# Splitting the last products by token tile, and three smaller moves at the end of an attention and feed-forward kernel

## The chip, the cores and the metric

The kernel runs on one core of a Trainium2 chip. The metric is the time of one execution on the device, in microseconds. Before the change the median of three runs was 293.77 us (293.49 to 294.30). The profile is of one execution, whose span from first to last instruction was 291.8 us, at the full granted TensorE clock.

Engine names in the profile: PE is TensorE's matmul, PEld its weight load, DVE is VectorE, ACT is ScalarE, POOL is GpSimd, SP is SyncE, which issues most of the transfers. L530 is line 530 of the kernel as it was before.

## The reference

There are two stages. The first is attention over 4 batches and 8 heads, 768 tokens, head dimension 64, in which a query sees only the keys whose six projected sign bits are the same as its own:

```python
q_bits = (np.einsum('bhsd,dk->bhsk', q, proj) > 0)
k_bits = (np.einsum('bhsd,dk->bhsk', k, proj) > 0)
# bits -> bucket number
mask = q_bucket[:, :, :, None] == k_bucket[:, :, None, :]
scores = np.where(mask, scale * np.matmul(q, k.transpose(0, 1, 3, 2)), -1e9)
attn = softmax(scores)
attn_out = np.matmul(attn, v)
```

The second takes the result as 3072 tokens of 512 values through a feed-forward block with a hidden width of 2048:

```python
h = x @ w_in                         # 3072 x 2048
g = h * (1.0 / (1.0 + np.exp(-h)))
out = g @ w_out                      # 3072 x 512
```

## The kernel before

The main loop runs over 288 units of attention (nine for each head). A unit w issues the scores of unit w + 3, an exponential on ScalarE, and the products with v of unit w. Between them a queue of feed-forward units for the previous batch is worked off. The last batch's feed-forward block follows in `tail`, with what is left in the queue as its filler.

```python
def score(w):
    ...
    sp = ps.tile([P, 512], F32, tag="s", name="s_ps", bufs=LEAD)      # LEAD = 3
    ... matmuls, L381
    nc.scalar.activation(out=u, in_=sp, func=AF.Exp, scale=ESC)       # L384
```

PSUM tiles come from three groups: "s" (three banks, for the scores), "m" (three banks, for the first matmul's result h_ps and other things) and "o" (two banks). The feed-forward block of a batch is cut into a chunk of 512 tokens (ci = 0) and one of 256 (ci = 1). The second matmul uses seven products in place of eight (Strassen's scheme in Winograd's form), so operands are first combined by additions. A feed-forward unit of the first matmul:

```python
hp = ps.tile([P, 2, f, n // 2], F32, tag="m", name="h_ps", bufs=3)
... matmuls, L478
nc.scalar.activation(out=th, in_=hp, func=AF.Tanh, scale=0.5)         # L488
def g_op():
    nc.vector.scalar_tensor_tensor(out=g, in0=th, scalar=1.0, in1=hp, ...)   # L491
after.append(g_op)
```

The combinations, and the products with the chain tile that they open:

```python
def comb(ci, n, f):
    ...
    eng = nc.gpsimd if n > 2 and scoring else nc.vector
    eng.tensor_tensor(out=dst, in0=x, in1=y, op=op)                   # L513

def product(ci, n, t):
    ...
    first = t == 0 and n in (1, 6, 7)
    if first:
        banks[ci, bank] = ps.tile([P, nt, NC], F32, tag="m" if in_head else "s" if scoring else "o",
                                  name="o2_ps", bufs=3 if in_head or scoring else 2)
    ... eight matmuls, L530
    ... copied by ScalarE (L540), or added to an earlier part by VectorE (L542); store, L551
```

`scoring` is true in the loop and false in `tail`. `in_head` is true for the first eleven units of the later batches. Chain n=1 serves products 1 and 2, n=6 serves 6, 5 and 3, n=7 serves 7 and 4. In `tail` the first matmul of the last batch comes from L687 (products 1, 6, 2, 7, 5, 3, 4 for each block of the hidden width), with copies by ScalarE at L698, additions by VectorE at L701, silu by ScalarE at L704, and combinations at L713 to L723. Then come the last products, in `last`, for a larger chunk (ci = 0, two token tiles) and a smaller one (ci = 1, one token tile):

```python
def last(ci, n, t, c0=0, c1=NC):
    ...
    if c0:
        i = 4
    first = t == 0 and n in (1, 6, 7)
    if first:
        bank["o", ci, i] = ps.tile([P, nt, NC], F32, tag="o" if c0 else "ms"[ci], ...)
    op = bank["o", ci, i]
    for k in range(NK):
        nc.tensor.matmul(op[:, t, c0:c1], a[:, cs], y[:, k, c0:c1], ...)    # L793
    if t < nt - 1:
        return
    ...
        nc.scalar.copy(out=o, in_=op)                                       # L807
    ... or
        nc.vector.tensor_tensor(out=o[:, :, c0:c1], in0=op[:, :, c0:c1],
                                in1=kept[ci, with_part][:, :, c0:c1], op=ALU.add)   # L809
    ...
    nc.sync.dma_start(out=dst[:, 3 * r + t0 : 3 * r + t0 + nt, :], in_=o[:, :, c0:c1])  # L821

for n in (1, -1, 6, -2, 2, -6, 5, -5, 7, 3, -3, -7, 4, -4):
    for t in range(2 if n > 0 else 1):
        for cols in ((0, 192), (192, NC)) if n in (-7, -4) else ((0, NC),):
            last(int(n < 0), abs(n), t, *cols)
```

A negative n is the smaller chunk. The end of the kernel is therefore: product 4 of the larger chunk, both token tiles; then product 4 of the smaller chunk, first 192 columns and then 64.

Of the kernel before, what the change touches and what calls it, by code (L numbers as in the profile page):

```python
# [13 lines left out]
ALU = mybir.AluOpType  # L14
# [3 lines left out]
def kernel(  # L18
# [10 lines left out]
    nc = tc.nc  # L29
# [137 lines left out]
    NC = DMODEL // 2  # L167
# [286 lines left out]
    def flush():  # L454
        for fn in after:
            fn()
        after.clear()

    def moe_units(b):
# [4 lines left out]
        def mm1(ci, grp, dts=slice(0, NDT)):  # L464

            c0, n, f = ((0, 512, 1), (512, 256, 2))[ci]
            ft0 = grp * f
            half = ft0 // NK
            if (ci, half) not in blk:
                blk[ci, half] = gpl.tile([P, 2, NK, n // 2], F16, tag=f"g{ci}{half}", name="g",  # L470
                                         bufs=2 if (ci, half) == (0, 1) else 1)
            hp = opened.pop((ci, grp), None)
            if dts.start == 0:
                hp = ps.tile([P, 2, f, n // 2], F32, tag="m", name="h_ps", bufs=3)
            for j in range(f):
                ft = ft0 + j
                for dt in range(dts.start, dts.stop):
                    nc.tensor.matmul(hp[:, :, j, :], w_in16[:, dt, ft * P : (ft + 1) * P],  # L478
                                     xT[4 * b + dt][:, c0 : c0 + n]
                                     .rearrange("d (r c) -> d r c", r=2),  # L480
                                     start=(dt == 0), stop=(dt == NDT - 1))
            if dts.stop < NDT:
                opened[ci, grp] = hp
                return
            k0 = ft0 % NK
            g = blk[ci, half][:, :, k0 : k0 + f, :].rearrange("p r f c -> p r (f c)")
            th = thp.tile([P, 2, f, n // 2], F32, tag="th", name="th")
            nc.scalar.activation(out=th, in_=hp, func=AF.Tanh, scale=0.5)  # L488

            def g_op():  # L490
                nc.vector.scalar_tensor_tensor(  # L491
                    out=g,
                    in0=th.rearrange("p r f c -> p r (f c)"), scalar=1.0,
                    in1=hp.rearrange("p r f c -> p r (f c)"),
                    op0=ALU.add, op1=ALU.mult)

            after.append(g_op)

        def comb(ci, n, f):

            if n == 3 and (ci, 3) not in blk:
                w = blk[ci, 0].shape[-1]
                blk[ci, 3] = gpl.tile([P, NK, w], F16, tag=f"g{ci}d", name="gd", bufs=1)
            a11, a21 = blk[ci, 0][:, 0, f], blk[ci, 0][:, 1, f]
            a12, a22 = blk[ci, 1][:, 0, f], blk[ci, 1][:, 1, f]
            dst, x, y, op = {1: (a21, a21, a22, ALU.add),
                             2: (a11, a21, a11, ALU.subtract),
                             3: (blk.get((ci, 3)), a22, a11, ALU.subtract),
                             4: (a12, a12, a11, ALU.subtract)}[n]
            if n == 3:  # L510
                dst = dst[:, f]
            eng = nc.gpsimd if n > 2 and scoring else nc.vector
            eng.tensor_tensor(out=dst, in0=x, in1=y, op=op)  # L513

        banks, kept = {}, {}
# [53 lines left out]
        def then(fn, *combs):  # L569

            def unit():
                fn()
                for c in combs:
                    after.append(lambda c=c: comb(*c))
            return unit

        lo, hi, al = slice(0, NK // 2), slice(NK // 2, NK), slice(0, NK)
        first = [lambda grp=grp: mm1(0, grp) for grp in range(NFT)]
# [15 lines left out]
        if b == 0:  # L594
            one = [[lambda grp=grp, dt=dt: mm1(0, grp, slice(dt, dt + 1)) for grp in range(2)]
                   for dt in range(NDT)]
            first = one[0] + one[1] + one[2] + one[3] + first[2:]
# [10 lines left out]
    def moe_head():  # L608
        units, late[:6] = late[:6], []
        return units  # L610

    def moe_list(b):


        first, second, big, small = moe_units(b) if b else first_units
        if b == 0:
            units = first + spread(second, big[:8])
            late[:] = big[8:] + small
            return units
        units = spread(first[:-3], late) + [big[0]] + first[-3:] + [big[1]]  # L620
        for i, c in enumerate("ababaababababa"):
            units.append((second, big)["ab".index(c)][("ababaababababa"[:i].count(c)) + 2 * (c == "b")])
        late[:] = big[8:] + small
        return units
# [22 lines left out]
    def tail(fill):  # L647
# [16 lines left out]
        def gb(r, c, k, n=1):  # L664
            t = G[2 * (2 * r + c) + k // 4]
            return t[:, k % 4 * NR0 : (k % 4 + n) * NR0]
# [106 lines left out]
        kept = {}  # L773

        def last(ci, n, t, c0=0, c1=NC):

            nt, t0 = ((2, 0), (1, 2))[ci]
            i, x, y = {1: (1, (0, 0), B11), 2: (1, (0, 1), B21),
                       6: (2, 2, wt[2]), 5: (2, (1, 0), wt[1]), 3: (2, 4, B22),
                       7: (3, 3, B12), 4: (3, (1, 1), wt[4])}[n]  # L780
            if c0:
                i = 4
            first = t == 0 and n in (1, 6, 7)
            if first:
                bank["o", ci, i] = ps.tile([P, nt, NC], F32, tag="o" if c0 else "ms"[ci],
                                           name="o2_ps", bufs=2 if c0 else 3)
            op = bank["o", ci, i]
            cs = slice((t0 + t) * P, (t0 + t + 1) * P)
            for k in range(NK):
                a = {2: s2[:, k], 4: s4[:, k],  # L790
                     3: s3[k // 2][:, k % 2 * NR0 : (k % 2 + 1) * NR0]}[x] \
                    if isinstance(x, int) else gb(x[0], x[1], k)
                nc.tensor.matmul(op[:, t, c0:c1], a[:, cs], y[:, k, c0:c1],  # L793
                                 start=(first and k == 0), stop=True, skip_group_check=True)
            if t < nt - 1:
                return
            with_part = {1: None, 2: None, 6: 1, 5: 1, 3: 1, 7: 5, 4: 6}[n]
            keep = n in (1, 6, 5)
            pool = nrm if keep else ops
            if not keep and ci == 0:  # L800
                pool = thp
            if c0 == 0:
                bank["out"] = pool.tile([P, nt, NC], F32, tag=f"part{ci}{n}" if keep else ("th", "osb")[ci],
                                        name="osb", bufs=1 if keep else 3)
            o = bank["out"]
            if with_part is None:
                nc.scalar.copy(out=o, in_=op)  # L807
            else:
                nc.vector.tensor_tensor(out=o[:, :, c0:c1], in0=op[:, :, c0:c1],  # L809
                                        in1=kept[ci, with_part][:, :, c0:c1], op=ALU.add)  # L810
            if keep:
                kept[ci, n] = o
                return
            if ci and n == 7:
                if c1 < NC:
                    return
                c0 = 0
            r, c = {2: (0, 0), 3: (0, 1), 7: (1, 1), 4: (1, 0)}[n]
            dst = out[b * S : (b + 1) * S, c * NC + c0 : c * NC + c1].rearrange(
                "(p t) n -> p t n", p=P)  # L820
            nc.sync.dma_start(out=dst[:, 3 * r + t0 : 3 * r + t0 + nt, :], in_=o[:, :, c0:c1])  # L821

        for n in (1, -1, 6, -2, 2, -6, 5, -5, 7, 3, -3, -7, 4, -4):
            for t in range(2 if n > 0 else 1):
# [4 lines left out]
    NW = NH * NU  # L829
    BST = 8 * NU  # L830
# [106 lines left out]
    scoring = True  # L937
    in_head = False
    for w in range(LEAD):
        score(w)  # L940
    for w in range(NW):
        flush()
        for fn in at.pop(w, []):
            fn()
        if w % BST == 1:
            moeq.extend(moe_head())
        if w == BST + 5 or w % BST == 11 and w > 2 * BST:
            credit = 0.5
            moeq.extend(moe_list(w // BST - 1))
        keep = 3 if w >= NW - 12 else 0  # L950
        left = BST - w % BST
        n = -(-(len(moeq) - keep) // left) if len(moeq) > keep else 0
        in_head = w > 2 * BST and w % BST < 11
        credit += max(len(moeq) - keep, 0) / left
        skip = credit < 0.999 or w % QST in ((20, 21) if w > 2 * BST else (24, 25))
        if w > 2 * BST and w % BST < 11:
            skip = w % BST in (0, 2, 5, 7, 10)
        if n == 1 and len(moeq) - keep < left and skip:
            n = 0
        credit -= n  # L960
        for _ in range(n):
            moeq.popleft()()
        av(w)
        if w + LEAD < NW:
            score(w + LEAD)
# [3 lines left out]
    for w in sorted(at):  # L969
        for fn in at[w]:  # L970
            fn()
    scoring = False
    act = nrm.tile([P, 1], F32, tag="act", name="act", bufs=1)
    nc.scalar.activation(out=act, in_=sc[:, 0:1], func=AF.Silu)
    tail(late)
# [28 lines left out]
```

## Time and profile before

| what | us |
|---|---|
| median of three runs | 293.77 |
| span in the profile | 291.8 |
| TensorE busy | 285.8 |
| ScalarE busy | 224.7 |
| GpSimd busy | 204.3 |
| VectorE busy | 202.8 |

The busy time of an engine is its own; engines work side by side, and what sets the end is the chain of work in which each step waited for the one before. In order of time the end of the kernel reads so: the scores end about 236 us, the first matmul of the last batch (L687) runs from 243.9 to about 270 us with fillers between, the last products (L793) from 269.8 to 288.3 us, then the last additions and the last three stores. The stretches near the end, with the busy time of each engine:

```profile
core 0: us, PE busy (x) PEld busy (x) DVE busy (x) ACT busy (x) POOL busy (x), PEclk, DMA share, GB/s
248.00:270.00 22.00, 22.00 (x155) 14.93 (x153) 16.61 (x34) 18.80 (x39) 9.73 (x6) 1.00 0.09 28
270.00:288.00 18.00, 18.00 (x179) 16.30 (x177) 6.71 (x14) 3.31 (x6) 3.24 (x2) 1.00 0.23 75
288.00:292.00 4.00, 0.32 (x10) 0.20 (x7) 0.62 (x3) 0.00 (x0) 0.00 (x0) 1.00 0.32 98
```

Each line is a stretch, its length, then the busy time and number of instructions of TensorE's matmul, its weight load, VectorE, ScalarE and GpSimd, then the granted clock, and the share and rate of the transfers.

### The profile page before, as it was taken

Reading aid. Unit: us, or ns where it says so; the run is one execution under the profiler, and the core shown is the slowest. Engines: PE = TensorE matmul, PEld = TensorE weight load, DVE = VectorE, ACT = ScalarE, POOL = GpSimd, SP = SyncE. Lnnn points to the kernel's source line nnn. Section 1 sums busy time; section 2 is a strip of 40 time slices with the busy share of each in tenths; the row PEclk is TensorE's granted clock in tenths of the full one; section 3 lists DMA queues with packets and bytes.
Section 4 is the critical chain, followed back from the end, with each engine's and each line's share of the span. In section 5 each row is a group of like instructions: output and inputs, shape, how many; then the busy total and the mean of one; then the engine's idle time right before and its main releaser. Section 6 shows DMA issues by size and latency. Waiting matters only on the chain.

```text
span 291.8 us, 7761 instructions
## 1 busy us (share of the span) xinstructions
PE 285.8 (98%) x2934; PEld 196.7 (67%) x2934; DVE 202.8 (70%) x402; ACT 224.7 (77%) x428; POOL 204.3 (70%) x241
## 2 busy tenths in 40 slices
PE   8999999999999999999999999999999999999995
PEld 3666765555666665566666888656668887666884
DVE  6788869898887465854897446965657659777332
ACT  5999999998988687777887786878888855788400
POOL 8789999379997956999257991589999850254400
PEclk9999999999999999999999999999999999999999
DMA  6999997969979359872288226203020212101114
GB/s 197 244 238 210 235 151 117 235 86 150 197 120 213 85 88 226 155 136 55 72 178 122 50 66 167 80 21 48 26 47 0 65 29 82 46 3 36 38 67 133
DMA packets 105861, 32.91 MB, mean 113 GB/s; under 512 B 90912, under 2 KB 105312, under 8 KB 105824
## 3 DMA queue, kind: packets, MB, share of 16 engines
q1 hardware_dynamic: 101440, 28.23, 46.9%
q0 software_dynamic: 4224, 4.19, 9.7%
q8 instruction: 23, 0.38, 0.6%
q14 instruction: 14, 0.11, 0.1%
q10 hardware_dynamic: 160, 0.00, 0.0%
HBM read 27.27 MB, written 6.29 MB: 115 GB/s over the span
## 4 chain that ended last, share of the span: by engine, by line
PE 92%; DVE 3%; ACT 2%; issue 1%; POOL 0%; DVEq 0%; ACTq 0%; POOLq 0%
PE h_ps L478 21%; PE s_ps L381 20%; PE o_ps L530 13%; PE o_ps L413 12%; PE o_ps L793 6%; PE h_ps L687 5%; PE o_ps L560 5%; PE bp_ps L295 3%; ACT u L384 2%; PE tp_ps L199 2%; PE warm_ps L125 1%; PE bp_ps L315 1%; DVE tx L660 1%; DVE osb L542 1%; PE bp_ps L239 1%
## 5 line engine op out<-in xcount | busy, mean ns | idle before, releaser
L384 ACT ACTIVATE u<-s_ps 128x512 f16<-128x512 f32 x288 | 156.9, 608 | 27.7 <-PE s_ps L381 27.1
L413 PEld LDWEIGHTS <-u 128*128 128x128 f16 x1152 | 67.3, 98 | 38.1 <-ACT u L384 9.4
L413 PE MATMUL o_ps<-vv,u 128*128 128x65 f16 x1152 | 82.5, 194 | 0.6 <-ACT u L384 0.4
L478 PE MATMUL h_ps<-xT,win 128*128 128x512 f16 (+1 forms) x384 | 75.1, 326 | 0.0
L491 DVE SCALAR_TENSOR_TENSOR g<-th,h_ps 128x512 f16<-128x512 f32 x72 | 48.4, 680 | 36.9 <-ACT th L488 36.4
L381 PE MATMUL s_ps<-qkb 128*128 128x512 f16 x192 | 53.1, 326 | 0.2 <-ACT u L384 0.2
L381 PE MATMUL s_ps<-qka 128*128 128x512 f16 x192 | 52.5, 326 | 0.2 <-DVE qka L252 0.2
L488 ACT ACTIVATE th<-h_ps 128x512 f32<-128x512 f32 x72 | 43.8, 608 | 10.3 <-PE h_ps L478 7.1
L478 PEld LDWEIGHTS <-win 128*128 128x128 f16 x384 | 37.5, 98 | 17.5
L530 PEld LDWEIGHTS <-g 128*128 128x128 f16 x336 | 32.8, 98 | 7.0 <-issue 0.3
L433 POOL TENSOR_TENSOR x_pr<-osum,rec 128x384 f16<-128x384 f32 x23 | 19.7, 857 | 22.3 <-DVE rec L432 21.2
L265 POOL TENSOR_SCALAR qka<-qk 64x1536 f16<-64x1536 f32 x15 | 21.9, 1462 | 15.6 <-DVE qk L260 9.2
L265 POOL TENSOR_SCALAR qkb<-qk 64x1536 f16<-64x1536 f32 x15 | 22.0, 1469 | 1.2
L530 PE MATMUL o_ps<-wt,g 128*128 128x256 f16 x168 | 21.8, 272 | 0.1
L530 PE MATMUL o_ps<-wout,g 128*128 128x256 f16 x168 | 21.4, 273 | 0.0
L276 POOL TENSOR_TENSOR vsa<-v_sb 128x192 f32<-128x192 f32 x32 | 18.9, 591 | 0.0
L274 POOL CAST vv<-v_sb 128x384 f16<-128x384 f32 x32 | 16.7, 521 | 0.5
L560 PE MATMUL o_ps<-wout,g 128*128 128x512 f16 x64 | 16.4, 379 | 0.0
L717 POOL TENSOR_TENSOR gs<-qka,gs 128x768 f16<-128x768 f16 x2 | 3.3, 1644 | 18.5 <-ACT qka L704 15.7
L260 DVE STREAM_TRANSPOSE qk<-k_blk 128x768 f32<-128x768 f32 x10 | 16.0, 1598 | 0.0
L381 PEld LDWEIGHTS <-qka 128*128 128x128 f16 x192 | 15.4, 97 | 0.8 <-ACT qka L252 0.6
L260 DVE STREAM_TRANSPOSE qk<-q_blk 128x768 f32<-128x768 f32 x10 | 15.9, 1588 | 0.0
(123 smaller groups left out, 441.6 us busy)
## 6 DMA issues: line engine op xcount, KB each, us to landing
v_sb<-in_v_dram SPq DMA_DIRECT2D x15, 384.0 KB
out_dram<-osb SPq DMA_DIRECT2D x16, 256.0 KB
q_blk<-in_q_dram SPq DMA_DIRECT2D x40, 96.0 KB
k_blk<-in_k_dram SPq DMA_DIRECT2D x40, 96.0 KB
win<-in_moe_w_in_dram POOLq DMA_DIRECT2D x4, 512.0 KB, 7.7
wout<-in_moe_w_out_dram POOLq DMA_DIRECT2D x4, 512.0 KB, 6.7
q_sb<-in_q_dram SPq DMA_DIRECT2D x5, 384.0 KB
k_sb<-in_k_dram SPq DMA_DIRECT2D x5, 384.0 KB
```

The source lines that it names most:

```text
L260: nc.vector.transpose(out=dst, in_=qk_sb[p, "qk"[n]])
L265: nc.gpsimd.tensor_scalar(out=dst[rows, :], in0=qk32[p][rows, :], scalar1=CS, scalar2=1.0, op0=ALU.mult, op1=ALU.mult)
L276: nc.gpsimd.tensor_tensor(out=sa, in0=src[:, 0:3], in1=src[:, 3:6], op=ALU.add)
L381: nc.tensor.matmul(sp[:, o0 : o0 + n], t[:, S + jt * P : S + (jt + 1) * P], t[:, c0 : c0 + n], start=True, stop=True)
L384: nc.scalar.activation(out=u, in_=sp, func=AF.Exp, scale=ESC)
L413: nc.tensor.matmul(o_ps[h][:, c0 // P + i, :], u[:, o0 + i * P : o0 + (i + 1) * P], vv[:, jt, :], start=(not direct(h) and w % NU == 0 and ...
L433: (nc.vector if direct(h) else nc.gpsimd).tensor_tensor(out=x_pr[p][:, :, par * D : (par + 1) * D], in0=o[:, 0:NJ, 0:D], in1=rec[:, :, Non ...
L478: nc.tensor.matmul(hp[:, :, j, :], w_in16[:, dt, ft * P : (ft + 1) * P], xT[4 * b + dt][:, c0 : c0 + n] .rearrange("d (r c) -> d r c", r=2 ...
L488: nc.scalar.activation(out=th, in_=hp, func=AF.Tanh, scale=0.5)
L491: nc.vector.scalar_tensor_tensor(out=g, in0=th.rearrange("p r f c -> p r (f c)"), scalar=1.0, in1=hp.rearrange("p r f c -> p r (f c)"), op ...
L530: nc.tensor.matmul(op[:, t, :], x[:, k, t * P : (t + 1) * P], y[:, k], start=(first and k == 0), stop=True, skip_group_check=True)
L560: nc.tensor.matmul(op, x, w_out16[:, ft, :], start=(ft == 0), stop=(ft == NFT - 1))
```

## The change

It has four parts, all near the end of the kernel.

1. The last two groups of the larger chunk (products 7 and 4) get a bank for each token tile, so that VectorE can add token tile 0 while TensorE works on token tile 1. The store still takes both token tiles.
2. The store of the first 192 columns of the very last product is issued from ScalarE's queue; the last 64 columns stay on SyncE's.
3. Two combinations of the smaller chunk (n = 4 and n = 3) that fall into the tail are given to GpSimd, so that VectorE is free for the additions of the tail.
4. Product chains opened from unit 268 on take a bank of the first matmul's group and not of the scores' group.

```diff
-            eng = nc.gpsimd if n > 2 and scoring else nc.vector
+            eng = nc.gpsimd if n > 2 else nc.vector
 ... in last():
-            if c0:
+            split = ci == 0 and n in (7, 4)
+            if c0 or split and t:
                 i = 4
-            first = t == 0 and n in (1, 6, 7)
+            first = n in (1, 6, 7) and (t == 0 or split)
 ...
-            if t < nt - 1:
+            if t < nt - 1 and not split:
                 return
+            ts = slice(t, t + 1) if split else slice(0, nt)
 ...
-            if c0 == 0:
+            if c0 == 0 and ts.start == 0:
                 bank["out"] = pool.tile(...)
 ...
-                nc.vector.tensor_tensor(out=o[:, :, c0:c1], in0=op[:, :, c0:c1],
-                                        in1=kept[ci, with_part][:, :, c0:c1], op=ALU.add)
+                nc.vector.tensor_tensor(out=o[:, ts, c0:c1], in0=op[:, ts, c0:c1],
+                                        in1=kept[ci, with_part][:, ts, c0:c1], op=ALU.add)
 ...
-            if ci and n == 7:
-                if c1 < NC:
+            if n == 7 or split:
+                if ci and c1 < NC or split and t == 0:
                     return
-                c0 = 0
+                c0, ts = 0, slice(0, nt)
 ...
-            nc.sync.dma_start(out=dst[:, 3 * r + t0 : 3 * r + t0 + nt, :], in_=o[:, :, c0:c1])
+            (nc.scalar if (ci, n, c0) == (1, 4, 0) else nc.sync).dma_start(
+                out=dst[:, 3 * r + t0 + ts.start : 3 * r + t0 + ts.stop, :], in_=o[:, ts, c0:c1])
 ... in the main loop:
-        in_head = w > 2 * BST and w % BST < 11
+        in_head = w > 2 * BST and w % BST < 11 or w >= NW - 20        # NW - 20 = 268
 ... after it:
-    scoring = False
+    scoring = in_head = False
```

## The prediction

> **What bounds the kernel now.** I read the page's busy shares first: TensorE is busy for 285.8 us of a span of 291.8 us, so there is little idle time to win back, and the question is where exactly it lies. I then read the waits with TensorE as the waiter, then the chain of work that ended last from 222 us to the end, then the timeline around each place where that chain leaves TensorE, and last the stretches after the final product.
>
> ```profile
> PE 285.8 (98%) x2934; PEld 196.7 (67%) x2934; DVE 202.8 (70%) x402; ACT 224.7 (77%) x428; POOL 204.3 (70%) x241
> ...
> PE h_ps L687 <- DVE part L701: 0.4, 1, 0.4
> PE s_ps L381 <- ACT u L384: 0.2, 1, 0.2
> ```
>
> These two are the only waits of its matmuls after 222 us. The chain shows what led to each:
>
> ```profile
> 231.13 0.60 ACT th L488
> 231.73 0.50 ACT u L384
> 232.22 0.04 issue
> 232.27 0.38 PE s_ps L381 x2
> ...
> 246.12 0.46 DVE g L513
> 246.58 0.06 issue
> 246.63 0.27 DVE gd L513
> 246.90 0.34 issue
> 247.24 0.56 DVE part L701
> 247.80 0.04 issue
> 247.84 1.14 PE h_ps L687 x6
> ...
> 269.94 18.16 PE o_ps L793 x176
> 288.11 0.03 issue
> 288.13 0.35 DVE osb L809
> ```
>
> A score tile had to wait for an exponential, which stood behind a tanh in ScalarE's order. Later TensorE waited for VectorE's addition at L701, which stood behind the two combinations of L513. From 247.84 to 288.11 us the chain holds TensorE alone: what reaches TensorE earlier by 247.84 us reaches the end earlier. The last fence shows how much is lost at each place, and what follows the last product:
>
> ```profile
> 231.77 0.28 PE L413 MATMUL o_ps<-vv,u 128*128 128x65 f16 x4
> 232.27 0.38 PE L381 MATMUL s_ps<-qkb 128*128 128x256 f16 x2 [0.21 <-ACT u L384]
> ...
> 246.68 0.81 PE L687 MATMUL h_ps<-tx,sw 128*128 128x384 f16 x4
> 247.84 0.65 PE L687 MATMUL h_ps<-tx,sw 128*128 128x384 f16 x3 [0.35 <-DVE part L701]
> ...
> 288.24 0.38 SPq L821 DMA_DIRECT2D out_dram<-osb  x1
> ...
> 288.72 0.42 SPq L821 DMA_DIRECT2D out_dram<-osb  x1
> ```
>
> The reader should see that a bracket is less than the loss. Matmuls overlap, so the cadence counts. Four of the 65-column products take 0.12 us in the chain: the score could have begun at 231.77 + 0.12 = 231.89 and began at 232.27, a loss of 0.38 us. Four 384-column products follow one another by 0.65 us (246.03 to 246.68 in the timeline): the next could have begun at 246.68 + 0.65 = 247.33 and began at 247.84, a loss of 0.51 us.
>
> [...] from 289.1 to 290.4 us the DMA share is 0.87 to 1.08 in each tenth (but the first, 0.40) at up to 369 GB/s, so the three last stores already fill the engines. [...] the combination that begins at 223.38 us, while GpSimd runs L645, takes 2.61 us, where those after 246 us with GpSimd idle take 0.68; the additions of L701, one input from PSUM, take 0.51 us each from 253.56 us beside GpSimd's L717. [...]
>
> **The change part by part.**
>
> Chains from unit 268. Working through the queue of the loop, I find three product chains of the last sequence: chain n=1 opens at unit 259, before the new limit; n=6 opens at unit 276; n=7 opens only in the tail. So one tile alone changes its bank. It opens at 228.51 us and is freed by the addition of n=3, at 242.44 + 0.68 = 243.12 us. Before, it takes one of three score banks, so only two scores can be in flight, and the score at 232.27 must wait for the exponential two before it (231.62 to about 232.2). With three, it needs the one before that, done at 230.99. Gain: 0.38 us. The cost would be in the first matmul: it keeps two banks instead of three until 243 us. Its tiles begin at 230.06, 234.03, 236.87 and 238.61 us; each needs the tile two before it to have been read by L491. Those reads end at about 229.04, 229.69, 232.94 and 236.42 us, each earlier than needed, by 1.0 us at the least. The opening itself needs a bank whose L491 ends at 227.58, 0.9 us early. So no new wait: 0.
>
> Two combinations on GpSimd. The only ones with n over 2 outside the scoring are those of the smaller chunk, n=4 and n=3, each 128x1024. They cost VectorE 0.68 us each, begun at 246.04 and 246.63. L701 then begins when product 2 of the first block ends, near 246.5, and ends near 247.1, before 247.33. That frees all 0.51 us. But the next bound is near: two products later TensorE needs bank 1 after ScalarE's copy (247.53 to 248.01), and would be there at 247.33 + 0.65 = 247.98. With the 0.04 us of a hand-over (the step at 247.80 in the chain), it starts at 248.05, so 0.07 us goes back. Gain: 0.51 - 0.07 = 0.44 us. GpSimd takes 2.12 us for each (the median of its L513 row), together 4.24, from about 245.2 to 249.5 us in the new order. Its next work is at 253.17, and the products that read the results come at 261.56 and 264.06. Both have room.
>
> Last products by token tile. TensorE does the same matmuls. VectorE does two additions of 128x256 (0.425 us each) instead of one of 128x512 (0.691), twice: 0.16 us more each, in a stretch in which it is busy 6.7 of 18 us. For n=7 nothing waits. For n=4 the last addition now takes 0.425 instead of 0.691, so the 256 KB store can be issued 0.27 us sooner: at about 287.97 instead of 288.24. Its own fourth bank of the matmul group was freed by the copy ending at 277.56, and is wanted at 281.13: no wait.
>
> Two queues. Before, issues begin at 288.24, 288.72 and 289.23 us. With the 96 KB store on ScalarE's queue, I expect 287.97, about 288.5 and about 288.65. The data flow from 289.15 to 290.42 us without a break. They move 384 KB in 1.27 us, so an earlier last issue doesn't shorten them; the flow's start is what counts, and that is the 0.27 us of the split. For the second queue I take 0.
>
> Sum: 0.38 + 0.44 + 0.27 = 1.09 us. The time is 293.77 - 1.09 = 292.68, which I state as 292.7 us.
>
> **The rivals.**
>
> First, the banks: with n=6 in a matmul bank, the first matmul of the smaller chunk could be what waits. For it: VectorE's reads of h_ps at L491 wait for the tanh by up to 2.4 us over the whole span, and a combination beside GpSimd took 2.61 us; one such delay in 229 to 236 us would use up the 1.0 us of room. Against it: the four dates above. It would give back up to 0.4 us: 293.1.
>
> Second, GpSimd stands in VectorE's way: a combination running into one of VectorE's with two SBUF inputs would lengthen that to as much as 2.6 us, and L713 to L715 feed silu's blocks and the last products. For it: the 2.61 us above. Against it: the tx combinations end by 245.52 (about 245.1 in the new order), where GpSimd begins, and L713 comes at 251.47 (about 250.7), over 1 us after GpSimd ends. If it happened: 0.5 to 1.5 us lost, 293.2 to 294.2.
>
> Third, the end is set elsewhere: the span ends 1.4 us after the last data, in completion that none of this touches, and the second queue may begin its flow later than expected, or have a longer completion. Then the end's 0.27 us is lost: 292.95. Or the issue does count, because the last 32 KB flow alone and slowly (41 to 244 GB/s in the last three tenths); then up to 0.3 us more is gained: 292.4.
>
> Fourth, a freed wait comes back: TensorE gets ahead and meets the next late producer. In the blocks after 250 us it meets the copy of ScalarE once in each, with about 0.08 us (253.48 + 8 x 0.1625 = 254.78, begun at 254.86); that is in the trace already and moves along. I see no other within 0.1 us.
>
> **Range and chances.** All three gains together are 0.4% of the time; no part can bring or cost 2% (5.9 us) by anything in the trace. The spread of the three times is 0.8 us, so the median may be off by 0.3 either way. Half of the gains lost gives 293.2; the end gaining 0.3 more gives 292.4. I take 292.1 to 293.4. Chances: 0.01 faster by over 2%, 0.98 within, 0.01 slower.
>
> **What would show each step.** Right: no wait of TensorE for u on the score line near 232 us, and none for part at L701 near 247; L513 in that place on GpSimd with about 2.1 us each; L701 beginning directly after product 2; the products of L793 beginning about 0.8 us earlier than 269.78; the last data flow beginning about 0.27 us nearer to the last product, still without a break, and about as long. Wrong: a TensorE wait on h_ps for L491, VectorE operations of 1 us or more between 245 and 252 us, a gap in the last flow, or a span that shrinks while TensorE's idle time does not.

## The result and the profile after

The changed kernel takes 292.58 us (median of six runs, 292.28 to 292.96), against 293.65 us before (six runs): 1.07 us less, a ratio of 0.9958 with a 95% interval of 0.9943 to 0.9973. In the table of busy times only GpSimd's has moved by more than 1 us, by the two combinations that it took over (204.3 to 208.5 us):

```profile
PE 285.7 (98%) x2934; PEld 196.7 (68%) x2934; DVE 202.3 (70%) x402; ACT 224.7 (77%) x428; POOL 208.5 (72%) x243
```

The chain of work that ended last, of the changed kernel (start, length, engine, tile, line):

```profile
232.00 0.21 PE s_ps L381
232.21 0.12 PE o_ps L413 x4
232.34 0.22 PE s_ps L381 x2
...
245.45 3.00 PE h_ps L687 x18
...
269.42 18.16 PE o_ps L794 x176
287.58 0.02 issue
287.60 0.36 DVE osb L811
```

Before, this chain left TensorE twice after 222 us, near 232 and between 239.7 and 247.8 us. Now it doesn't leave it at all before the last addition: the 18 products of L687 from 245.45 us on follow one another through the place where TensorE had stood still, and no matmul after 222 us has a wait in the list of waits. L794, L811 and L823 are the earlier L793, L809 and L821. The timeline of the changed kernel shows how:

```profile
245.53 2.13 POOL L513 TENSOR_TENSOR g<-g 128x1024 f16<-128x1024 f16 x1 [7.80 <-PE o_ps L530]
...
246.53 1.02 DVE L701 TENSOR_TENSOR part<-h_ps,part 128x384 f32<-128x384 f32 x2 [0.50 <-PE h_ps L687]
246.58 1.46 PE L687 MATMUL h_ps<-tx,sw 128*128 128x384 f16 x8
...
247.96 0.48 PE L687 MATMUL h_ps<-xT,sw 128*128 128x384 f16 x2
...
286.94 0.42 DVE L811 TENSOR_TENSOR osb<-o_ps,osb 128x256 f32<-128x256 f32 x1 [0.39 <-PE o_ps L794]
```

L701 now waits for TensorE, and not TensorE for L701. The eight products of 0.1625 us each would end their turn at 246.58 + 1.30 = 247.88, and the next begins at 247.96: the 0.08 us that ScalarE's copy costs in each block. The last line is the addition of token tile 1 alone, 0.42 us long.

One caution in comparing the two profiles by the clock: TensorE reaches the product with v ahead of the first of these places at 232.05 us here and at 231.77 before, so 0.28 us were lost earlier in this execution, where the program hasn't changed. I therefore compare distances between instructions, not dates. From this product with v to the first of the last products (L793, now L794) it is 269.78 - 231.77 = 38.01 us before and 269.25 - 232.05 = 37.20 us now, 0.81 us less, where the prediction's first two terms are 0.82; in a second profile of the changed kernel it is 37.20 us again. The spans (291.8 and 291.0 us) differ by only 0.8 because of the 0.28 us; that of the second profile was 290.6 us.

### The profile page after: what moved, and what is told of

Read it like the earlier page. It is cut to its first block, busy times and chain, and to the rows that moved or that the text cites. A ratio compares the mean times of both kernels' runs of the same rounds, so it can differ in the third digit from the quotient of the medians.

```text
span 291.0 us, 7769 instructions
## 1 busy us (share of the span) xinstructions
PE 285.7 (98%) x2934; PEld 196.7 (68%) x2934; DVE 202.3 (70%) x402; ACT 224.7 (77%) x428; POOL 208.5 (72%) x243
## 4 chain that ended last, share of the span: by engine, by line
PE 95%; ACT 2%; issue 1%; DVE 1%; POOL 0%; DVEq 0%; ACTq 0%; POOLq 0%
PE h_ps L478 21%; PE s_ps L381 20%; PE o_ps L530 15%; PE o_ps L413 13%; PE h_ps L687 6%; PE o_ps L794 6%; PE o_ps L560 5%; PE bp_ps L295 3%; ACT u L384 2%; PE tp_ps L199 2%; PE warm_ps L125 1%; PE bp_ps L315 1%; PE bp_ps L239 1%; PE tp_ps L212 1%; PE o_ps L404 0%
## 5 line engine op out<-in xcount | busy, mean ns | idle before, releaser
L513 POOL TENSOR_TENSOR g<-g 128x1024 f16<-128x1024 f16 x7 | 15.2, 2188 | 7.8 <-PE o_ps L530 7.8
L701 DVE TENSOR_TENSOR part<-h_ps,part 128x384 f32<-128x384 f32 x24 | 12.6, 555 | 5.1 <-PE h_ps L687 3.0
```

## The experiments

### Each part alone

Four kernels took one part of the change each.

Banks alone:

```diff
-        in_head = w > 2 * BST and w % BST < 11
+        in_head = w > 2 * BST and w % BST < 11 or w >= NW - 20
-    scoring = False
+    scoring = in_head = False
```

> Only the fourth part: chains from unit 268 take a matmul bank. My theory (three separate waits, each worth its own term): TensorE's wait for u near 232 us is gone, the wait for part at L701 near 247 us stays with its loss of 0.51 us, the last flow of stores starts as long after the last product as before; 0.38 us less than before, about 293.3 against 293.65. Rival (the freed wait comes back in another place, since h_ps has one bank less): a TensorE wait for L491 between 230 and 239 us, and 0 to 0.1 us less than before.

Measured: 293.17 us (21 runs), ratio 0.9987 (0.9979 to 0.9996). The list of TensorE's waits after 200 us has one line left, the one near 247 us:

```profile
PE h_ps L687 <- DVE part L701: 0.3, 1, 0.3
```

In the timeline the product with v is followed by the score after 0.12 us, where it took 0.50 before (231.77 to 232.27): 0.38 us gained, as expected, and no wait in another place.

```profile
231.65 0.29 PE L413 MATMUL o_ps<-vv,u 128*128 128x65 f16 x4
231.77 0.38 PE L381 MATMUL s_ps<-qkb 128*128 128x256 f16 x2
```

The rival of the lost matmul bank falls.

Combinations alone:

```diff
-            eng = nc.gpsimd if n > 2 and scoring else nc.vector
+            eng = nc.gpsimd if n > 2 else nc.vector
```

> Only the third part: two tail combinations on GpSimd. My theory: the wait near 247 us is gone, and the block that follows starts 0.44 us sooner with 0.07 us of the 0.51 going to ScalarE's copy; the wait near 232 us stays; 0.44 us less than before, about 293.2. Rival (GpSimd hinders VectorE): operations of VectorE of 1 us or more between 245 and 250 us and 0.2 us gained at most.

Measured: 293.33 us (13 runs), ratio 0.9987 (0.9978 to 0.9996). Here the other line is left:

```profile
PE s_ps L381 <- ACT u L384: 0.2, 1, 0.2
```

The same stretch of TensorE, from the first products of L687 with tx to the first with xT after them, takes 247.52 to 248.90 = 1.38 us; before it took 246.68 to 248.49 = 1.81. That is 0.43 us gained. In this kernel, and then the end of the stretch before:

```profile
247.52 1.46 PE L687 MATMUL h_ps<-tx,sw 128*128 128x384 f16 x8
248.90 0.48 PE L687 MATMUL h_ps<-xT,sw 128*128 128x384 f16 x2
...
248.49 0.49 PE L687 MATMUL h_ps<-xT,sw 128*128 128x384 f16 x2
```

VectorE's additions beside the two GpSimd operations (246.46 to 250.68 us) take 1.02 us for two, as without them.

Split alone, with all stores on one queue:

```diff
+            split = ci == 0 and n in (7, 4)
 ... (the other lines of the change in last(), but not the ScalarE queue)
```

> Only the first part: products 7 and 4 of the larger chunk by token tile, all stores on one queue. My theory: the flow of the last stores is bound by its start, so it starts 0.27 to 0.32 us nearer to the last product and takes about as long as before (1.27 us); both waits of TensorE stay; 0.3 us less than before, about 293.35. Rival (the last issue counts): without the second queue the last issue still comes about 1.1 us after the last product's end, the flow gets a gap or a thin end, and nothing or 0.1 us is gained.

Measured: 293.30 us (13 runs), ratio 0.9994 (0.9985 to 1.0002). By the times alone this isn't clear of nothing; by the profile the end has moved, see the table below.

Two queues alone:

```diff
-            nc.sync.dma_start(out=dst[:, 3 * r + t0 : 3 * r + t0 + nt, :], in_=o[:, :, c0:c1])
+            (nc.scalar if (ci, n, c0) == (1, 4, 0) else nc.sync).dma_start(
+                out=dst[:, 3 * r + t0 : 3 * r + t0 + nt, :], in_=o[:, :, c0:c1])
```

> Only the second part: the 96 KB store on ScalarE's queue. My theory: the last issue moves from 289.23 to about 288.72 us, but the flow starts at the same distance from the last product and moves the same 384 KB, so nothing is gained: 0 to 0.06 us. Rival (the last issue sets the end): up to 0.3 us less than before.

Measured: 293.58 us (13 runs), ratio 1.0001 (0.9993 to 1.0009). Nothing gained, as expected.

For the end of the kernel I take as zero the begin of VectorE's addition of the last 192 columns (the last VectorE step of the chain: 288.13 us before, 287.60 us in the changed kernel). The trace says when the last data packet ends, which stretches of 0.01 us show too, and when the last instruction of the core ends:

| kernel | data stop, us after zero | core ends, us after zero |
|---|---|---|
| before | 2.36 | 3.67 |
| changed | 2.04 | 3.37 |
| split alone, one queue | 2.05 | 3.36 |
| two queues alone | 2.37 | 3.67 |

The split moves the end of the data by 0.32 us and the end of the core by 0.31; the second queue moves neither by more than 0.01, with the split or without it. In all four the data flow without a gap for about 1.36 us. The first of the last three stores is issued at 288.24 us before, 0.11 us after zero, and in the changed kernel 0.21 us before zero:

```profile
287.39 1.06 SPq L823 DMA_DIRECT2D out_dram<-osb  x2
```

The kernels of this set shared 49 runs of before. Medians are 0.46, 0.30, 0.33 and 0.05 us below theirs (293.63), together 1.14. The runs of one kernel spread over 0.6 to 1.1 us (all but one of those of before), so the median depends a little on where they happen to fall; the lowest runs (before 293.39; 293.03, 292.95, 293.09, 293.40) give 0.36, 0.44, 0.30 and -0.01, together 1.09. Either sum is close to the change's 1.07. The times alone don't resolve more than that: the ratios above multiply to 0.9969, about 0.9 us, and 0.9958 of the whole change is within their joint uncertainty. That the parts add rests on the distances in the profiles: 0.38, 0.43 and 0.31 us one by one, and 0.81 (the first two) and 0.31 us together.

### Does it matter where the GpSimd operations lie?

The changed kernel with one more tail combination on GpSimd:

```diff
-            eng = nc.gpsimd if n > 2 else nc.vector
+            eng = nc.gpsimd if n > 2 or n == 2 and not scoring else nc.vector
```

> The changed kernel with a third tail combination (n = 2 of the smaller chunk) on GpSimd too. It begins about 241.7 us, just before VectorE's eight combinations tx (L660), which have two inputs in SBUF; the two that the change moved begin after tx is done. If where they lie decides (my theory): tx is held up until GpSimd is done, about 243.9 us, the blocks of L687 that read tx wait, and 0.4 to 1.0 us of the gain is lost: 293.0 to 293.6. Rival (a GpSimd operation does not hinder VectorE, or VectorE has room here): tx ends as before or sooner, and the time is that of the changed kernel, 292.6, within 0.1.

Measured: 298.64 us (4 runs), ratio 1.0164 (1.0151 to 1.0177). The direction is the expected one, the size is not: about 6 us above the changed kernel, not 0.4 to 1.0. The timeline of this kernel, first GpSimd, then VectorE, then TensorE:

```profile
241.37 2.13 POOL L513 TENSOR_TENSOR g<-g 128x1024 f16<-128x1024 f16 x1 [4.04 <-DVE g L513]
245.18 2.12 POOL L513 TENSOR_TENSOR g<-g 128x1024 f16<-128x1024 f16 x1 [1.69 <-PE o_ps L530]
247.26 2.23 POOL L513 TENSOR_TENSOR gd<-g 128x1024 f16<-128x1024 f16 x1
...
242.41 1.30 DVE L660 TENSOR_TENSOR tx<-xT 128x384 f16<-128x384 f16 x1
...
245.21 2.30 DVE L660 TENSOR_TENSOR tx<-xT 128x384 f16<-128x384 f16 x1
247.44 2.27 DVE L660 TENSOR_TENSOR tx<-xT,tx 128x384 f16<-128x384 f16 x1
...
250.82 1.40 PE L687 MATMUL h_ps<-tx,sw 128*128 128x384 f16 x4 [2.61 <-DVE part L701]
```

A tx combination takes 0.35 us elsewhere in this trace. The first is held until 243.71, just after the added GpSimd operation ends at 243.50. That pushes the last two back into the two operations that the change had moved, which begin 0.03 and 0.18 us ahead of them. All three end 0.21 or 0.22 us after the GpSimd operation beside them, and take 1.30, 2.30 and 2.27 us. Both inputs of a tx combination are in SBUF. The additions of L701, with one input from PSUM, weren't lengthened by GpSimd: two take 1.02 us beside it in the changed kernel, and 1.02 us with GpSimd idle here (255.19 us). What holds the one kind and not the other, no trace shows. L701 comes after the tx combinations in VectorE's order, and TensorE waits for it.

The second half of the loss is in the windows of the same kernel (length, then busy time of TensorE's matmul, weight load, VectorE, ScalarE and GpSimd, then the granted clock):

```profile
247.50:250.90 3.40, 0.72 (x4) 0.36 (x4) 3.40 (x5) 0.48 (x1) 1.99 (x1) 1.00 0.00 0
250.90:254.30 3.40, 3.40 (x14) 1.99 (x14) 1.36 (x3) 1.70 (x3) 0.00 (x0) 0.50 0.35 116
254.30:256.00 1.70, 1.70 (x13) 1.01 (x12) 0.81 (x2) 1.13 (x3) 0.00 (x0) 1.00 0.00 0
```

After the stall TensorE's granted clock is 0.50 for 3.4 us: 14 matmuls fill 3.40 us there, and 13 the 1.70 us that follow at 1.00. By the distance from the first product of L687 with tx to the one that waited for L701, it lost 4.0 us to waiting (5.95 us, 244.87 to 250.82, against 1.95 in the changed kernel: 245.28 to 246.58 + 0.65). Half the clock for 3.4 us is 1.7 us more, an estimate from the granted clock. Together 5.7 us. In the profiles the way from that first product to the first of L794 is 5.78 us longer than in the changed kernel (244.87 to 274.62 against 245.28 to 269.25); the medians differ by 6.06.

### Is one matmul bank less ever felt?

The changed kernel with the limit brought down by 41 units, so that every chain of the last sequence that opens in the loop takes a matmul bank:

```diff
-        ... or w >= NW - 20
+        ... or w >= NW - 61
```

> The changed kernel with the limit of unit 268 brought down to unit 227, so that all chains of the last sequence take a bank of the first matmul's group. It asks whether one bank less for h_ps costs anything. My theory: chains at unit 229 to 259 hold a bank while VectorE is behind (a combination of 1.4 to 2.6 us beside GpSimd near 222 to 226 us), so a wait of TensorE for L491 shows up there, 0.2 to 0.8 us in all: 292.8 to 293.4. Rival (two banks are enough everywhere): no wait, and as fast as the changed kernel, 292.6 within 0.1.

Measured: 292.67 us (5 runs), ratio 0.9964 (0.9952 to 0.9976). My expectation was wrong and its rival right: TensorE has no wait after 200 us in this kernel either, and the time is the changed kernel's. In this run two banks were enough for h_ps in all of the last sequence.

### A shorter end?

If the last flow is bound by its 384 KB, it should help to store token tile 0 of product 4 as soon as it is added. In both kernels below the larger chunk's product 4 is stored in two pieces of 128 KB; the first is called e7 in the expectations, and the second also keeps all stores on SyncE's queue.

```diff
-            if n == 7 or split:
+            if n == 7:
                 if ci and c1 < NC or split and t == 0:
                     return
```

> The changed kernel with product 4 of the larger chunk stored by token tile too, 128 KB each, the last stores on two queues. My theory: the last flow was bound by its 384 KB; with 128 KB of them gone before the last product it is bound by the last issue: it ends about 0.9 us after the issue at 0.5 us behind the last product, some 0.3 to 0.4 us sooner than in the changed kernel: 292.2 to 292.3. Rival (the end is set by the completion after the last issue, whatever it moves): less than 0.15 us gained.

> As e7, but with all stores on one queue. If the amount of data no longer binds (my theory), the last issue now counts: it comes about 0.4 to 0.5 us later than with two queues, so 0.3 to 0.5 us of time more than e7, about 292.6. Rival (the second queue never counts): as e7 within 0.1 us.

Measured: 292.86 us (22 runs, ratio 0.9976, 0.9966 to 0.9986) and 292.90 us (22 runs, 0.9974, 0.9962 to 0.9985). Neither is faster than the changed kernel, and the queue again makes no difference in the time, as the rival of the second expectation had it. I ran the changed kernel, the first of these again and two more on one chip. The two more join the last 96 KB and 32 KB into one store of 128 KB, with product 4 of the larger chunk stored whole, and by token tile:

```diff
 ... one store at the end:
-            if n == 7 or split:
+            if n == 7 or split or ci and n == 4:
 ... one store at the end, and product 4 by token tile:
-            if n == 7 or split:
+            if n == 7 or ci and n == 4:
```

> The changed kernel again, on the same chip as the three that follow: about 1.1 us less than before, 0.9962; the last data end about 1.97 us after VectorE's addition of the last 192 columns begins, and the core's end follows about 1.4 us later.

> e7 again (product 4 of the larger chunk stored by token tile), beside the changed kernel on one chip. In e7 the data ended sooner (1.82 us after that addition begins) but the end of the core followed 1.77 us after them, not 1.4. If that belongs to the kernel (stores whose data do not queue behind others take as long from issue to completion anyway), it is seen again, and the time is 0.1 to 0.3 us above the changed kernel's. If it was chance, the end follows after 1.4 us and the time is 0.15 us below.

> The changed kernel with the two last stores (96 KB and 32 KB) made one of 128 KB, issued by ScalarE after the addition of the last 64 columns. Two issues are left at the end. If the amount of data and the last issue set the end: data end about 1.8 us after the addition of 192 columns begins, 0.15 us less time than the changed kernel. If the completion of small stores costs (the 32 KB in rows of 256 bytes): up to 0.4 us less. If the earlier start of the 96 KB counts: as the changed kernel or up to 0.2 us more.

> Both: product 4 of the larger chunk stored by token tile, and one 128 KB store at the end. If the completion after a gap in the flow is what made e7 slow, it is as slow here as e7 or more, 0.1 to 0.3 us above the changed kernel; if the thin last store did it, it is 0.1 to 0.4 us below.

| kernel (stores of L823) | time, us | ratio | data stop | core ends | difference |
|---|---|---|---|---|---|
| changed, again (9) | 292.39 | 0.9963 | 2.06 | 3.37 | 1.31 |
| by token tile, two queues, first run (10) | 292.86 | 0.9976 | 1.87 | 3.60 | 1.73 |
| the same, again (10) | 292.70 | 0.9972 | 1.86 | 3.59 | 1.73 |
| by token tile, one queue (10) | 292.90 | 0.9974 | 1.98 | 3.67 | 1.69 |
| one last store (8) | 292.43 | 0.9967 | 1.98 | 3.29 | 1.31 |
| both (9) | 292.32 | 0.9965 | 1.90 | 3.16 | 1.27 |

Columns four and five count from the same zero as above; the expectations give 1.82 and 1.97 us for two of the ends of the data, where the trace has 1.87 and 2.06. Storing by token tile does end the data 0.2 us sooner, less than the 0.3 to 0.4 that I had expected: the data now come in three pieces with gaps between them, and the last piece begins only 1.28 us after zero. Three parts of the expectations failed: the time, the amount, and the queue, which I had thought would count here (0.3 to 0.5 us; it counts 0.1 in the data's end). But the core ends 0.4 us later after its data, in three of three profiles, so it is the kernel's and not chance. A gap in the flow isn't its cause by itself: the last kernel of the table has the gap and ends 1.27 us after its data. A thin last store isn't either: the changed kernel has it and needs 1.31.

The traces show where the 0.4 us go. After a store's data they have updates of one semaphore (16 for the last store of the changed kernel, 289.86 to 290.05 us), and I call the last of them its report. At the end SyncE makes nine waits for semaphores, of two each and in the same order before and after the change. In the changed kernel the last store is reported at 290.05 us, 0.40 us after its last data, and its semaphore stands in the last of the nine waits. With ten stores in the tail the last one takes an earlier transfer's semaphore again, which stands in the second wait. It is reported as soon after its data (289.58 to 289.99 us), but seven waits still follow. Counted from just before the report, in the changed kernel and then in that by token tile:

```profile
L1002 SPq EVENT_SEMAPHORE  x1: 28/28/28, 290.1 to 290.1; - x1
...
L1002 SPq EVENT_SEMAPHORE  x8: 27/28/28, 290.0 to 290.4; - x8
```

They come every 0.06 us, so the seven are 0.43 us. From the report to the end of the core it is 1.33 to 1.35 us in the three profiles with ten stores and 0.90 to 0.92 with nine; with eight, where one wait follows, it is 0.96. So it is the count of the stores, and neither the gap nor the thin store. This is read from traces of kernels made for another question; no kernel tests it alone.

The last kernel of the table has nine stores and the early data, and the shortest end in the profile (3.16 us, 0.21 less than the changed kernel's). It has the lowest median too, but 0.07 us below the changed kernel is less than these runs resolve. No version beats the change clearly.

## Why the prediction was right

The prediction said 292.7 us, and 292.58 was measured; as a difference, 1.09 us less was predicted and 1.07 measured. That the sums lie so close is in part luck: the interval of the measured ratio stands for anything from 0.8 to 1.7 us less, and the median before was 293.77 us in the three runs that the prediction started from and 293.65 in six. What carries the account is that each term was found by itself:

- **Banks, 0.38 us.** 0.38 in the timeline of that part alone. That one chain tile alone moves, and that it costs h_ps nothing, held; the limit at unit 227 shows that the room was larger than the dates had told.
- **Combinations, 0.51 - 0.07 = 0.44 us.** 0.43 in the part alone. Both terms are right: the lost cadence was 0.51 us, where the bracket of the wait said only 0.35, and the copy of ScalarE took back 0.08.
- **Split, 0.27 us.** The data stop 0.32 us sooner and the core ends 0.31 us sooner. The sum left out that the addition of token tile 1 also begins a little earlier: 0.66 us before zero and no longer 0.61. The store's issue moved from 0.11 us after zero to 0.21 before it, 0.32 in all. The kernel gives token tile 1 a bank of its own; whether the early addition would need it, no run shows.
- **Second queue, 0.** No gain in the part alone (1.0001), none in the data's end with or without the split. The reason given, a flow without a break whose start counts, is what the profile shows; only its length was read a little short, 1.27 us for 1.36.
- **The rivals.** The bank that h_ps misses: not seen, even with all chains moved. GpSimd in VectorE's way: not in the change, as the dates said; but the delay is real (2.30 us for 0.35 in one tx combination), and one more combination 4 us earlier costs 6 us. The last issue that counts: not in the change, and with 128 KB of the data stored earlier it moves their end by 0.1 us and the time by nothing that these runs resolve. A freed wait that comes back: the 0.08 us of the copy and nothing else.

What the prediction could not have told is the size of the second rival: it put 0.5 to 1.5 us on a collision. It didn't reckon with the delay pushing further operations into collisions, nor with the clock.

## What to carry to other kernels

When TensorE is busy for nearly the whole span (98% here), list its few waits and read the loss from the cadence of its instructions, not from the bracket of the wait: pipelined matmuls hid about a third and nearly half of it here (0.35 for 0.51 us, 0.21 for 0.38 us). Work moved to GpSimd cost nothing here beside additions with one input from PSUM (1.02 us for two of L701, with GpSimd busy or idle), and about 6 us where it met combinations with both inputs in SBUF (2.30 us for 0.35); look at the dates of both before moving it, and at what a delay would push into them. For the last flow of stores, which ran without a gap here, the first issue counted (0.31 us) and a second queue didn't (0.01 us at most). When stores are split, count them: two kernels that ended their data sooner ended later, by the traces because the tenth store was waited for in another place, with seven waits of 0.06 us behind it.

## What the runs showed that I had not expected

A single stall was followed by half the clock. In the kernel with the third combination a wait of 2.61 us, in a stretch of 3.4 us with 0.72 us of matmul (21%), was followed by 3.4 us at a granted clock of 0.50, full of matmuls, and these by the full clock.

The clock records show how long such stretches are and how busy they were. In the profiles before and after the change the clock is full for 286.72 us from its first record on, which is 84 times 3.413 us; in the kernel with the third combination it is half from 250.90 to 254.31 us, once this length. At the ends of the kernels, where TensorE finishes, stretches of this length are partly busy. In the changed kernel 1.65 us of matmul from 286.15 to 289.56 us were followed by the full clock; in the first kernel stored by token tile 1.41 us from 286.50 to 289.91 us were followed by half. So for these two the difference lies between 41 and 48% of the stretch. Whether it also matters where in a stretch a stall falls, no run shows.

And the end of a core didn't follow its last data by a fixed time here: 1.27 to 1.32 us in nine of the profiles, and 1.69 to 1.73 us in the three with ten stores in the tail, where seven more waits come after the last report.
